# Window attention and a squared-ReLU feed-forward: three of four second-stage groups of the last pair of tiles as Strassen's seven products of 256 columns

## The chip, the cores and the metric

One core of one Trainium2 chip. The metric is device time in microseconds, here of that one core. The core's engines run side by side, each from its own queue in order: TensorE (PE, matmuls; PEld are its weight loads), VectorE (DVE), ScalarE (ACT), GpSimd (POOL), and SyncE (SP), which here issues every DMA.

## The reference

Windowed attention, then a feed-forward layer on its output, in float32:

```python
def _attn_ref(q, k, v):                      # 8 batches, 8 heads, 576 tokens, 64 wide; window 64
    scores = np.matmul(q, k.transpose(0, 1, 3, 2)) / np.sqrt(D)
    scores = np.where(mask, scores, -1e9)    # mask: 0 <= row - column < 64
    attn = np.exp(scores - np.max(scores, axis=-1, keepdims=True))
    attn = attn / (np.sum(attn, axis=-1, keepdims=True) + 1e-09)
    return np.matmul(attn, v)

def _moe_ref(x, w_in, w_out):                # x: 4608 x 512, w_in: 512 x 2048, w_out: 2048 x 512
    r = np.maximum(x @ w_in, 0.0)
    return (r * r) @ w_out
```

## The kernel before

**Tiles.** The 4608 tokens are 12 tiles of 384. float32 operands are split into a high part and a rest (`hi`, `lo`), and a product is three matmuls: hi by hi, hi by the other's rest, rest by hi. The first four tiles are computed plainly. The other eight are four pairs, j = 0 to 3, and the attention of a later pair runs beside the feed-forward of an earlier one; the last pair has no attention beside it.

**First stage of a pair** (x @ w_in): Strassen's scheme with seven products. `product(s, n)` (L896), s = 0 to 31, n = 0 to 6, eight steps s for a pair (`NP` = 8), does 6 matmuls of 384 columns into a PSUM bank of a ring of four (`bank`, L891, PSUM banks 4 to 7). DVE and ACT combine the seven sums into four blocks of g, and square them (`square`, L926; which engine does it stands in `SQUARES`, L956). The first half of the tokens lands in `g_first` (L618), a ring of three, the second half in `g_last` (L623), a ring of four in the slabs gb0 and gb1.

**Second stage** (g @ w_out): `second(k, x)` (L959) runs two steps behind. Two steps k, k + 1 make a group; an even k does the first half of the tokens for the group's 512 rows of w_out, an odd k the second. For each of three blocks x of 128 tokens: an ACT copy to `high(c)` (L609), a DVE subtraction to `low(c)` (L612), 12 matmuls of 512 columns into one bank (L991), and a DVE addition to `parts` (L602, by ACT's copy in the first group of a pair). `high` and `low` are thirds, 512 columns each, of the slabs hi and lo. The fourth group's sums go out by DMA (L1002).

**Weights.** `kept` and `mixed` are tensors in DRAM: the split weights, and Strassen's combinations of w_in, made by `mixing` (L841) ahead of the pairs. `wi_fetch` (L718) fetches 256 KB for a product into one of 13 slots, `wo_fetch` (L726) 512 KB of w_out into one of 8. Each waits, in SP's queue, until the slot is free and a tick (a product that PE has done) has come.

**Order.** `Plan` (L638) collects the operations with estimated costs, reads, writes and places. PE's order is that of the program. `in_order` (L655) orders the other engines' queues beforehand: at each point the ready operation with the earliest due time, which it counts back from PE's order. Waits at run time come from the data.

The main loop runs s = 0 to 33: products of s, fetches, then `second(s - 2, x)`, with bursts of attention between.

Of the kernel before, what the change touches and what calls it, by code (L numbers as in the profile page):

```python
# [8 lines left out]
F32 = mybir.dt.float32  # L9
F32R = mybir.dt.float32r  # L10
# [19 lines left out]
def window_attention_relu2_ffn(ctx: ExitStack, tc: tile.TileContext, q, k, v, w_in, w_out, out):  # L30
# [485 lines left out]
    mixed = dram.tile([NF // 2, P, 4, 2, 2 * P], F32, name="mixed")  # L516

# [118 lines left out]
    NP = NF // 2  # L636

# [88 lines left out]
    def wo_fetch(name, f, tick):  # L726
        n = wo_n[0]
        wo_n[0] += 1
        slot = n % NWO
        wo[name] = slot  # L730
        plan("sp", 0.4, lambda: sp.dma_start(wo_slot(slot).bitcast(F32), kept[f, :, 1]), tick, [("wo", slot)], 3.5,
             freed(f"wo{slot // 2}") if n < NWO else [], 1.4)
# [163 lines left out]
    def product(s, n):  # L896
# [20 lines left out]
        g11, g21 = ((lambda m=m: g_first(s % 3)[:, m], [("ga", s % 3, m)]) for m in range(2))  # L917
        g12, g22 = ((lambda m=m: g_last(s % 4)[:, m], [("gb", s % 4, m)]) for m in range(2))
        first_a = [("ghi", m) for m in range(3)] + [("glo", m) for m in range(2)] if s < 3 else []
        first_b = freed(f"gb{s % 4 // 2}") if s < 4 else []  # L920
# [16 lines left out]
        if n == 0:  # L937
            plan("act", 0.5, lambda: act.copy(sc(), b[0][:, :TT]), [b[1]], ["sc"], 0, first_s)
        elif n == 1:
            add(v, [kv], a[0][:, :TT], a[1], sc, "sc")  # L940
        elif n == 2:
            add(u, [ku], c[0][:, :TT], c[1], v, kv, first_s)
        elif n == 3:
            add(lambda: by_half(g22[0]()), g22[1], ordered(d[0][:, :TT]), d[1], lambda: ordered(u()), ku, first_b)
            square(g22, False, SQUARES[0])
        elif n == 4:
            plan("act", 0.5, lambda: act.activation(by_half(g11[0]()), ordered(a[0][:, :TT]), AF.Relu), [a[1]], g11[1], 0, first_a)  # L947
            square(g11, True, SQUARES[1])
        elif n == 5:
            add(lambda: by_half(g21[0]()), g21[1], ordered(c[0][:, :TT]), c[1], lambda: ordered(v()), kv, first_a)  # L950
            square(g21, False, SQUARES[2])
        elif n == 6:
            add(lambda: by_half(g12[0]()), g12[1], ordered(d[0][:, :TT]), d[1], lambda: ordered(v()), kv, first_b)
            square(g12, False, SQUARES[3])

    SQUARES = "dve", "pool", "pool", "dve"  # L956
    split_n = [0]

    def second(k, x):  # L959
# [3 lines left out]
        size, name = (4, "gb") if half else (3, "ga")  # L963
# [4 lines left out]
        def src():  # L968
            if half:
                g_last(slots[0])  # L970
                all4 = slabs[f"gb{slots[0] // 2}"][:, :4 * TT].rearrange("p (a b c) -> p a b c", a=2, b=2)
            else:
                g_first(0)
                all4 = xs["g"][:, slots[0]:slots[1] + 1:slots[1] - slots[0]]
            return all4[:, :, :, x * P:(x + 1) * P]
        g_keys = [(name, slot, m) for slot in slots for m in range(2)]
# [4 lines left out]
        plan("act", 0.62, lambda: act.copy(high(c), src()), g_keys, [kh], 0, freed("hi") if new else [])  # L981
        plan("dve", 0.7, lambda: dve.tensor_tensor(low(c), src(), high(c).bitcast(F32), ALU.subtract), g_keys + [kh], [kl], 0,
             freed("lo") if new else [])
# [9 lines left out]
        plan("pe", 2.59, do, [kh, kl] + [("wo", y) for y in w], [key])  # L993
# [10 lines left out]


# [31 lines left out]
    for s in range(NP * FULL + 2):  # L1037
        if s < NP * FULL:
            for mark in marks.get(2 * s, []):
                mark()  # L1040
            for n in range(7):
# [3 lines left out]
                if s % 2 == 0 and n % 2 == 0:  # L1045
                    f = s % NP * 2 + n // 2
                    wo_fetch((s // NP, f), f, [("tick", s, n)])
        if s >= 2:
# [45 lines left out]
```

## Time and profile before

| | |
|---|---|
| median of 3 runs | 849.41 us (848.75 to 849.77) |
| span of the profiled execution, first to last instruction | 847.5 us |
| PE busy | 830.3 us, 98% |
| DVE, ACT, POOL busy | 70%, 48%, 22% of the span |
| granted TensorE clock, mean | 0.998 |
| last pair of tiles | from 711.46 us |

The page gives no total for the profiled execution beside its span. PE counts as busy while a matmul is anywhere in its pipeline, so what a matmul costs is read from the time of a block divided by its matmuls, not from the mean duration of one. "Idle before" is the time in which the engine did nothing before the instructions of a group, with what ended it.

### The profile page before, as it was taken

What the parts mean: (1) busy time and instruction counts of PE and PEld (TensorE: products, weight loads), DVE (VectorE), ACT (ScalarE), POOL (GpSimd) and SP (SyncE); (2) the same over time, 40 slices, a digit from 0 to 9 for tenths busy, and PEclk for the clock granted to TensorE, in tenths of its full rate; (3) what the DMA queues carried; (4) which work ended last, traced back from release to release, by engine and by line L of the source; (5) the groups of instructions that cost most, each with busy time, mean ns of one, the idle gap of its engine ahead of it and who ended that gap; (6) DMA issues with size and microseconds to landing.
All of it is one profiled execution on the core that took longest, in us unless ns stands there. A gap on an engine that the chain in (4) does not pass through costs nothing.

```text
span 847.5 us, 17708 instructions
## 1 busy us (share of the span) xinstructions
PE 830.3 (98%) x6754; PEld 761.5 (90%) x6754; DVE 593.2 (70%) x888; ACT 406.3 (48%) x1130; POOL 184.4 (22%) x237
## 2 busy tenths in 40 slices
PE   7799999999999999999999999999999999999998
PEld 6678988989999999999999999999999999999997
DVE  4999996567766867867777765788755668544553
ACT  5896764645546554544452354353455324222221
POOL 1220003114457520311230121141112131011110
PEclk9999999999999999999999999999999999999999
DMA  9989954736698884998896797999785555776411
GB/s 225 225 250 360 306 238 77 146 84 173 175 191 265 216 178 111 296 255 209 185 323 240 172 220 159 281 230 264 219 235 151 195 189 179 242 256 213 133 69 75
DMA packets 273011, 173.92 MB, mean 205 GB/s; under 512 B 190496, under 2 KB 239648, under 8 KB 270880
## 3 DMA queue, kind: packets, MB, share of 16 engines
q1 hardware_dynamic: 272928, 172.80, 73.4%
q8 instruction: 53, 0.87, 0.4%
q14 instruction: 30, 0.25, 0.1%
HBM read 138.15 MB, written 34.60 MB: 204 GB/s over the span
## 4 chain that ended last, share of the span: by engine, by line
PE 86%; DVE 5%; DMA 3%; SPq 3%; ACT 2%; issue 1%; POOL 0%; DVEq 0%; ACTq 0%; POOLq 0%
PE banks L991 29%; PE banks L910 26%; PE banks L446 10%; PE banks L404 10%; PE banks L235 4%; PE banks L298 3%; SPq L147 3%; DMA w<-in_moe_w_out_dram 2%; PE banks L276 2%; DMA kept<-w 1%; PE banks L196 1%; DVE a L125 1%; DVE w L132 1%; DVE pt L280 1%; ACT a L118 1%
## 5 line engine op out<-in xcount | busy, mean ns | idle before, releaser
L991 PE MATMUL banks<-w 128*128 128x512 f32 x1152 | 257.5, 380 | 0.0
L991 PEld LDWEIGHTS banks<-w 128*128 128x128 f32 x1152 | 215.7, 189 | 28.4
L404 PE MATMUL banks<-x,w 128*128 128x384 f32 x768 | 138.1, 330 | 2.1 <-ACT r L413 2.0
L446 PE MATMUL banks<-w,g 128*128 128x512 f32 x576 | 136.4, 382 | 0.1
L404 PEld LDWEIGHTS banks<-x,w 128*128 128x128 f32 x768 | 126.7, 190 | 6.8 <-ACT r L413 3.6
L910 PE MATMUL banks<-x,w 128*128 128x384 f32 x768 | 130.3, 326 | 0.0
L936 POOL TENSOR_TENSOR g<-g 128x384 f32<-128x384 f32 x64 | 58.3, 913 | 324.4 <-ACT g L947 309.5
L910 PEld LDWEIGHTS banks<-x,w 128*128 128x128 f32 x768 | 125.6, 189 | 0.0
L446 PEld LDWEIGHTS banks<-w,g 128*128 128x128 f32 x576 | 106.2, 189 | 14.1 <-DVE g L423 0.9
L263 ACT ACTIVATE sel<-sel,nm 128x64 f32<-128x64 f32 x272 | 90.8, 336 | 23.1 <-DVE nm L257 22.8
L910 PE MATMUL banks<-w 128*128 128x384 f32 x576 | 100.7, 329 | 0.0
L999 DVE TENSOR_TENSOR w<-w,banks 128x512 f32<-128x512 f32 x72 | 49.5, 687 | 69.1 <-PE banks L991 69.1
L910 PEld LDWEIGHTS banks<-w 128*128 128x128 f32 x576 | 93.8, 189 | 1.9
L413 ACT ACTIVATE r<-banks 128x384 f32<-128x384 f32 x64 | 31.3, 489 | 71.9 <-PE banks L404 66.7
L981 ACT CAST w<-w 128x512 fp32r<-128x512 f32 x48 | 29.8, 620 | 72.9 <-PE banks L991 72.9
L272 POOL TENSOR_TENSOR sel<-sel,nm 128x512 f32<-128x512 f32 x33 | 36.0, 1091 | 109.6 <-ACT g L947 51.7
L981 ACT CAST w<-g 128x512 fp32r<-128x512 f32 x48 | 29.7, 621 | 62.1 <-PE banks L991 60.0
L263 ACT ACTIVATION_READ_ACCUMULATOR sel<-sel,nm 128x1 f32 x272 | 51.2, 188 | 0.0
L423 DVE TENSOR_TENSOR g<-r,g 128x384 fp32r<-128x384 f32 x64 | 37.2, 584 | 17.3 <-ACT g L421 11.3
L929 DVE SCALAR_TENSOR_TENSOR w<-w 128x384 f32<-128x384 f32 x64 | 46.8, 731 | 1.8
L924 DVE TENSOR_TENSOR w<-banks,r 128x384 f32<-128x384 f32 x64 | 38.6, 603 | 13.1 <-PE banks L910 12.9
L280 DVE TENSOR_TENSOR pt<-banks,masks 128x1024 f32<-128x1024 f32 x33 | 40.2, 1219 | 10.6 <-PE banks L276 10.6
(103 smaller groups left out, 970.6 us busy)
## 6 DMA issues: line engine op xcount, KB each, us to landing
w<-mixed SPq DMA_DIRECT2D x128, 256.0 KB, 5.2
w<-kept SPq DMA_DIRECT2D x64, 512.0 KB, 7.2
w<-kept SPq DMA_DIRECT2D x96, 256.0 KB, 5.7
kept<-w SPq DMA_DIRECT2D x16, 1024.0 KB, 9.2
vt<-in_v_dram SPq DMA_DIRECT2D x144, 64.0 KB, 3.1
w<-in_moe_w_in_dram SPq DMA_DIRECT2D x16, 512.0 KB, 7.2
w<-in_moe_w_out_dram SPq DMA_DIRECT2D x16, 512.0 KB, 8.1
raw<-in_q_dram SPq DMA_DIRECT2D x112, 72.0 KB, 3.1
```

What stands on the lines that cost most here:

```text
L263: act.activation(sels[i][:, w, hd], sels[i][:, w, hd], AF.Exp, bias=nms[i][:, n], scale=SCALE, accum_out=sums[i][:, n])
L280: dve.tensor_tensor(pts[i].rearrange("p (w n) q -> p w n q", n=2), ps_t[i][:, :, None, :].broadcast_to([P, SW, 2, P]), masks.rearrange("p ...
L404: pe.matmul(h_ps, lhsT=weights(kk, part), rhs=in_turn(x[xx][:, kk // 2, kk % 2]), start=n == 0, stop=n == 3 * NK - 1)
L423: (pool if eng == "p" else dve).tensor_tensor(gs[n][1], rg.pop(n), gs[n][0].bitcast(F32), ALU.subtract)
L446: pe.matmul(acc(t, tb), lhsT=gg[:, ts], rhs=in_turn(weights(part)), start=f == 0 and n == 0, stop=f == NF - 1 and n == 2)
L910: pe.matmul(ps[:, :TT], lhsT=w[:, part, kk * P:(kk + 1) * P], rhs=in_turn(x[:, xx, kk]), start=n < 4 and m == 0, stop=m == 5, skip_group_c ...
L924: plan("dve", 0.6, lambda: dve.tensor_tensor(to(), ps, other(), ALU.add), [kps, ko], keys, 0, after)
L929: plan("dve", 0.57, lambda: dve.scalar_tensor_tensor(x(), x(), 0.0, x(), ALU.max, ALU.mult), [], keys)
L936: plan("pool", 0.95, lambda: pool.tensor_tensor(x(), x(), x(), ALU.mult), [], keys)
L981: plan("act", 0.62, lambda: act.copy(high(c), src()), g_keys, [kh], 0, freed("hi") if new else [])
L991: pe.matmul(ps, lhsT=gg[:, m // 2, m % 2], rhs=in_turn(wo_slot(w[m])[:, part]), start=m == 0 and n == 0, stop=m == 3 and n == 2)
L999: plan("dve", 0.72, lambda: dve.tensor_tensor(by_half(parts(tb)), by_half(parts(tb)), ordered(ps), ALU.add), [key], [kp])
```

## The change

In the last pair (s = 24 to 31, `LAST` = 24), three groups (k = 24, 26, 28) no longer run `second`. `fast_half(k)` builds Strassen's operands from the 2 x 2 blocks of g (a11 and a12 the first half of the tokens, a21 and a22 the second): sums in the slab t (DVE three, POOL one), and for each of seven operands an ACT copy and a DVE subtraction of 768 columns into one of four sets of buffers (`side`; sets 0 and 1 lie in the slabs hi and lo, two others in tiles of the attention). `fast(k, m)` runs a product: 3 token blocks x 2 x 3 matmuls of 256 columns, into two PSUM banks of 0 to 3, which are evacuated into `total(m)`, by ACT's copy for k = 24, by a DVE addition after. Products 0 to 3 run after the products of s = k + 2, products 4 to 6 after those of s = k + 3. `fast_out` combines the seven totals into `parts` in s = 31, and the fourth group (k = 30, 31) is done by `second` as before, with its fetches of w_out ticked in s = 31 in place of s = 30. `mixing2(j, p, c)` makes w_out's combinations, by POOL, ACT and DVE, in pairs j = 1 and 2 (p = 0 to 5, c = 0, 1: twelve times) and writes them to `mixed2` in DRAM. `fast_fetch` fetches each product's weights, from `kept` by two DMAs or from `mixed2` by one. In the last pair `LAST_SQUARES` gives two of four squares to ACT in place of DVE, and `g_first` lies in the tile `wide`, a ring of four.

```diff
+    mixed2 = dram.tile([NF // 2, P, 4, 2, DM // 2], F32, name="mixed2")
...
+    def g_first(s):
+        return g_steps()[:, s % 3] if s < LAST else wide()[:, s % 4 // 2, s % 2]
...
+    LAST = NP * (FULL - 1)
+    SETS = 4
...
+    LAST_SQUARES = "act", "pool", "pool", "act"
...
+        dead = [(y, c) for y in ("shi", "slo") for c in range(2)] if k >= LAST else []
+        plan("act", 0.62, lambda: act.copy(high(c), src()), g_keys, [kh], 0, freed("hi") if new else dead)
...
+    def mixing2(j, p, c):
...
+        for f in range(2):
+            plan("pool", 0.81, by(whole, f), wo_keys([w[f]]), [("m2", f)])
+        both = [("m2", f) for f in range(2)]
+        for to, a, b in (((0, 0), (0, 1), (0, 0)), ((0, 1), (1, 1), (0, 1)), ((1, 1), (1, 1), (0, 0)), ((1, 0), (1, 1), (1, 0))):
+            plan("pool", 0.54, by(less, to, a, b), [], both, 1.0 if to == (1, 0) else 0.0)
+        plan("act", 0.62, lambda: act.copy(top(), scr()), both, ["m2hi"], 1.0)
+        plan("dve", 0.7, lambda: dve.tensor_tensor(scr().bitcast(F32R), scr(), top().bitcast(F32), ALU.subtract), ["m2hi"], both)
+        for part, x, keys in ((0, top, ["m2hi"]), (1, scr, both)):
+            plan("sp", 0.5, lambda part=part, x=x: sp.dma_start(
+                mixed2[p, :, :, part, c * P:(c + 1) * P], x().bitcast(F32).rearrange("p f l c -> p (f l) c")),
+                 keys, [("mixed2", p, c, part)], 4.5, (), 0.9)
+
+    FAST = ("A11", 0, 0), ("A12", 1, 0), ("A22", 2, None), ("S1", 0, None), ("S2", 3, None), ("S4", 1, 1), ("S3", 1, None)
...
+    def side(n):
...
+        if n < 2:
+            views = [slab(name, F32R)[:, n * 2 * TT:(n + 1) * 2 * TT] for name in ("hi", "lo")]
+        elif n == 2:
+            views = [xs[name][:, :2 * TT] for name in ("sel", "pt")]
+        else:
+            views = [xs["vt"][:, part * 2 * TT:(part + 1) * 2 * TT] for part in range(2)]
...
+        def split(name, x):
+            n = side_n[0] % SETS
...
+            plan("act", 0.84, lambda: act.copy(side(n)[0], x[0]()), x[1], [("shi", n)], 0, dead)
+            plan("dve", 0.97, lambda: dve.tensor_tensor(side(n)[1], x[0](), side(n)[0].bitcast(F32), ALU.subtract),
+                 x[1] + [("shi", n)], [("slo", n)], 0, dead)
+        split("A11", a11)
+        split("A12", a12)
+        split("A22", a22)
+        mixed_of("dve", t[0], a21, a22, ALU.add)
+        mixed_of("pool", t[1], a11, a21, ALU.subtract)
+        split("S1", t[0])
+        fast(k, 0)
+        mixed_of("dve", t[0], t[0], a11, ALU.subtract)
+        split("S2", t[0])
+        fast(k, 1)
+        mixed_of("dve", t[0], a12, t[0], ALU.subtract)
+        split("S4", t[0])
+        fast(k, 2)
+        split("S3", t[1])
+        fast(k, 3)
...
+    def fast(k, m):
...
+        pair = fast_n[0] % 2
+        fast_n[0] += 1
+        ps = banks[:, 2 * pair:2 * pair + 2].rearrange("p a b -> p (a b)")[:, :2 * TT]
...
+            for x in range(NTB):
+                c = 0
+                for st in range(2):
+                    for gg, part in ((hi, 0), (hi, 1), (lo, 0)):
+                        pe.matmul(ps[:, x * 2 * P:(x + 1) * 2 * P], lhsT=gg[:, st, x * P:(x + 1) * P], rhs=in_turn(w[:, st, part]),
+                                  start=c == 0, stop=c == 5, skip_group_check=True)
+                        c += 1
...
+        if k == LAST:
+            plan("act", 0.84, lambda: act.copy(total(m), ps), keys, to, 0,
+                 QK_KEYS if m < 6 else [("ga", n, y) for n in range(3) for y in range(2)])
+        else:
+            plan("dve", 0.97, lambda: dve.tensor_tensor(total(m), total(m), ps, ALU.add), keys, to)
...
+        write("pool", 0, 0, M1, M2, ALU.add)
+        inside("dve", M6, M1, ALU.add)
+        inside("pool", M3, M5, ALU.add)
+        write("dve", 0, 1, M6, M3, ALU.add)
+        inside("dve", M7, M6, ALU.add)
+        write("dve", 1, 0, M7, M4, ALU.subtract)
+        write("dve", 1, 1, M7, M5, ALU.add)
+
+    FAST_FIRST = 4
+    FAST_END = NP * FULL - 2
...
-                if s % 2 == 0 and n % 2 == 0:
...
+                if s < LAST and s % 2 == 0 and n % 2 == 0 or s == FAST_END + 1 and n % 2 == 0:
...
+                if s > LAST and s % 2 and n % 2 == 0 and s < FAST_END:
+                    fast_fetch(s - 1, n // 2, [("tick", s, n)])
+                if s > LAST + 1 and s % 2 == 0 and n % 2:
+                    fast_fetch(s - 2, FAST_FIRST + n // 2, [("tick", s, n)])
+        if LAST + 2 <= s < FAST_END + 2:
+            if s % 2 == 0:
+                fast_half(s - 2)
+            else:
+                for m in range(FAST_FIRST, 7):
+                    fast(s - 3, m)
+            if s == FAST_END + 1:
+                fast_out()
+        elif s >= 2:
+            if NP + 2 <= s < NP * 3 + 2 and (s - 2) % NP < NP - 2:
+                mixing2((s - 2) // NP, (s - 2) % NP, (s - 2) // NP - 1)
```

## Rows read from the trace of the kernel before

**Rows 1.** The page: busy time, share of the span and instructions of each engine, and the granted clock of PE in 40 slices, in tenths.

```profile
PE 830.3 (98%) x6754; PEld 761.5 (90%) x6754; DVE 593.2 (70%) x888; ACT 406.3 (48%) x1130; POOL 184.4 (22%) x237
...
PEclk9999999999999999999999999999999999999999
```

**Rows 2.** The chain of waits of the last pair of tiles, in order of time: start, duration, what, how many.

```profile
711.46 6.83 PE banks L910 x42
718.28 7.77 PE banks L991 x36
...
820.45 23.32 PE banks L991 x108
...
843.79 0.69 DVE w L999
```

**Rows 3.** A window of two steps in the last pair, k = 24 in the second stage: from and to, length, busy time of PE, PEld, DVE, ACT and POOL (with instructions), granted clock, DMA share and GB/s.

```profile
740.65:769.84 29.19, 29.19 (x158) 27.26 (x158) 13.73 (x21) 8.87 (x17) 3.32 (x4) 1.00 0.63 207
```

**Rows 4.** Groups by line and shape of PE and PEld in the last pair, 711.46 to 843.8 us: busy time, mean ns of one, idle time before.

```profile
L991 PE MATMUL banks<-w 128*128 128x512 f32 x360 | 79.0, 379 | 0.0
...
L991 PEld LDWEIGHTS banks<-w 128*128 128x128 f32 x360 | 67.8, 189 | 9.2
```

**Rows 5.** Matmuls of 128 columns: the timeline of PE's warm-up matmuls from 11.7 us (start, duration from the first one's start to the last one's end, count), their loads and matmuls by line (ns, least, median, most), and four transposes from the chain of waits.

```profile
11.48 1.95 PE L512 MATMUL banks<-ident 128*128 128x128 f32 x16
...
L512 PEld LDWEIGHTS banks<-ident x58: 190/192/333, 1.5 to 24.3; 128*128 128x128 f32 x58
L512 PE MATMUL banks<-ident x58: 273/275/579, 1.5 to 24.4; 128*128 128x128 f32 x58
...
643.67 0.44 PE banks L276 x4
```

**Rows 6.** Groups by line and shape of DVE and ACT in the last pair.

```profile
L999 DVE TENSOR_TENSOR w<-w,banks 128x512 f32<-128x512 f32 x25 | 17.2, 688 | 31.2 <-PE banks L991 31.2
L929 DVE SCALAR_TENSOR_TENSOR w<-w 128x384 f32<-128x384 f32 x18 | 12.4, 690 | 0.6
L982 DVE TENSOR_TENSOR w<-w 128x512 fp32r<-128x512 f32 x15 | 10.3, 686 | 6.0 <-ACT w L981 6.0
L924 DVE TENSOR_TENSOR w<-banks,r 128x384 f32<-128x384 f32 x16 | 9.7, 608 | 5.0 <-PE banks L910 5.0
...
L924 DVE TENSOR_TENSOR g<-banks,r 128x384 f32<-128x384 f32 x8 | 5.2, 648 | 5.7 <-PE banks L910 5.7
L924 DVE TENSOR_TENSOR w<-banks,w 128x384 f32<-128x384 f32 x8 | 5.2, 648 | 2.9 <-PE banks L910 2.9
L924 DVE TENSOR_TENSOR r<-banks,w 128x384 f32<-128x384 f32 x8 | 4.5, 558 | 4.2 <-PE banks L910 4.0
...
L981 ACT CAST w<-w 128x512 fp32r<-128x512 f32 x15 | 9.3, 620 | 24.3 <-PE banks L991 24.3
...
L932 ACT ACTIVATE g<-g 128x384 f32<-128x384 f32 x8 | 4.2, 525 | 9.3 <-DVE g L924 9.3
```

**Rows 7.** Operations of 768 columns: groups of DVE, ACT and POOL from 380 to 711 us; and, from the timelines of DVE and POOL, a DVE operation that begins while POOL squares.

```profile
L874 DVE TENSOR_TENSOR w<-a,w 128x768 fp32r<-128x768 f32 x6 | 5.7, 949 | 0.0
...
L873 ACT CAST x<-w 128x768 fp32r<-128x768 f32 x6 | 5.0, 834 | 0.2
...
L862 POOL TENSOR_TENSOR w<-a,w 128x768 f32<-128x768 f32 x3 | 5.5, 1831 | 0.2
...
705.16 1.58 DVE L862 TENSOR_TENSOR w<-a,w 128x768 f32<-128x768 f32 x1
...
705.06 0.86 POOL L936 TENSOR_TENSOR g<-g 128x384 f32<-128x384 f32 x1 [1.28 <-ACT g L932]
```

**Rows 8.** Windows, columns as in rows 3: the densest stretch of DVE, and steps 10 to 15 (pair j = 1) and 18 to 23 (pair j = 2).

```profile
437.00:453.00 16.00, 16.00 (x89) 15.03 (x88) 15.48 (x23) 7.99 (x13) 2.30 (x2) 1.00 0.68 210
483.00:566.00 83.00, 83.00 (x693) 76.59 (x690) 57.54 (x94) 37.31 (x126) 19.60 (x18) 1.00 0.84 218
614.00:697.00 83.00, 83.00 (x700) 76.53 (x693) 49.91 (x84) 35.14 (x112) 18.53 (x17) 1.00 0.63 197
```

**Rows 9.** Timeline: the start of the last plain blocks on PE with the first copy and addition behind them, and a wait of PE for an evacuation by ACT earlier in the run.

```profile
820.28 23.47 PE L991 MATMUL banks<-w 128*128 128x512 f32 x108
...
822.91 0.62 ACT L981 CAST w<-g 128x512 fp32r<-128x512 f32 x1 [2.20 <-PE banks L991]
823.07 0.69 DVE L999 TENSOR_TENSOR w<-w,banks 128x512 f32<-128x512 f32 x1 [1.04 <-PE banks L991]
...
189.11 0.49 ACT L413 ACTIVATE r<-banks 128x384 f32<-128x384 f32 x1 [2.31 <-PE banks L404]
...
189.65 0.76 PE L404 MATMUL banks<-x,w 128*128 128x384 f32 x3 [0.58 <-ACT r L413]
```

**Rows 10.** Groups of POOL over the whole span: the sums of `mixing`, of 256 and 128 columns.

```profile
L539 POOL TENSOR_TENSOR a<-a 128x128 f32<-128x128 f32 x56 | 29.3, 541 | 1.4
L535 POOL TENSOR_TENSOR a<-w 128x256 f32<-128x256 f32 x28 | 25.0, 909 | 99.5 <-DVE w L132 73.7 <-DVE a L543 25.7
...
L535 POOL TENSOR_TENSOR w<-w 128x256 f32<-128x256 f32 x4 | 2.9, 731 | 2.0 <-DVE w L543 1.5 <-PE banks L446 0.5
```

**Rows 11.** DMA: issues of w_out's fetches from 711.46 to 828 us (count, KB each, median us from issue to landing), and what SP's queue waited for before a w_in fetch from 430 to 844 us (us in total, times, longest).

```profile
w<-kept SPq DMA_DIRECT2D x16, 512.0 KB, 7.0
...
SPq L723 <- PE banks L910: 133.7, 76, 10.9
```

More of the change, by code (lines that the diff above doesn't have):

```diff
@@ L971, in src @@
                 all4 = slabs[f"gb{slots[0] // 2}"][:, :4 * TT].rearrange("p (a b c) -> p a b c", a=2, b=2)
-            else:
-                g_first(0)
-                all4 = xs["g"][:, slots[0]:slots[1] + 1:slots[1] - slots[0]]
+            elif k >= LAST:
+                all4 = wide()[:, slots[0] // 2]
+            else:
+                all4 = g_steps()[:, slots[0]:slots[1] + 1:slots[1] - slots[0]]
             return all4[:, :, :, x * P:(x + 1) * P]
-        g_keys = [(name, slot, m) for slot in slots for m in range(2)]
+        g_keys = [key for s in pairs for m in range(2) for key in ([("gb", s % 4, m)] if half else g_first_keys(s, m))]
         c = split_n[0] % 3
@@ L1002, in second, with whole, less @@
             plan("sp", 0.4, lambda: sp.dma_start(out[row:row + P, :], parts(tb)), [kp], [], 3.0, (), 0.7)
+    def mixing2(j, p, c):
+        w = [wo[j, 2 * p + f] for f in range(2)]
+        scr = lambda: slab("gb0", F32)[:, 3 * DM:].rearrange("p (f l c) -> p f l c", f=2, l=2)
+        top = lambda: slab("gb1", F32)[:, 3 * DM:].bitcast(F32R).rearrange("p (f l c) -> p f l c", f=2, l=2)
+        def whole(f):
+            hi, lo = (wo_slot(w[f])[:, part].bitcast(F32).rearrange("p (l c) -> p l c", l=2)[:, :, c * P:(c + 1) * P]
+                      for part in range(2))
+            pool.tensor_tensor(scr()[:, f], hi, lo, ALU.add)
+        def less(to, a, b):
+            x = scr()
+            pool.tensor_tensor(x[:, to[0], to[1]], x[:, a[0], a[1]], x[:, b[0], b[1]], ALU.subtract)
+        for f in range(2):
[9 more added lines that the diff above has]
+                 keys, [("mixed2", p, c, part)], 4.5, (), 0.9)
@@ new lines, in window_attention_relu2_ffn, with fast_fetch @@
+    FAST = ("A11", 0, 0), ("A12", 1, 0), ("A22", 2, None), ("S1", 0, None), ("S2", 3, None), ("S4", 1, 1), ("S3", 1, None)
+    def fast_fetch(k, m, tick):
+        p = k % NP
+        name, kind, half = FAST[m]
+        if half is None:
+            source = [mixed2[p:p + 2, :, kind].rearrange("s p h e -> p s (h e)")]
+            keys = [("mixed2", p + n, c, part) for n in range(2) for c in range(2) for part in range(2)]
+        else:
+            source = [kept[2 * (p + n) + kind, :, 1, :, half * 2 * P:(half + 1) * 2 * P] for n in range(2)]
+            keys = []
+        wo_fetch(("fast", k, m), source, whole_slot if half is None else both_slot, keys + tick)
```

104 lines of the change are left out of this document (87 added, 17 removed).

## The prediction

> **What bounds it now.** I read the engine shares and slices first: TensorE (PE) is busy 98% of the span at full granted clock [rows 1]. Then the chain of waits over the last pair of tiles: from 711.46 us it holds matmuls alone, products (L910) and second-stage blocks (L991) in turn, until 843.77, with one VectorE (DVE) add and the output's DMA behind [rows 2]. A window of two steps agrees: PE busy 29.19 of 29.19 us, DVE 47%, ScalarE (ACT) 30%, GpSimd (POOL) 11% [rows 3]. So in this stage the time is the number of matmuls times their spacing. A block of 36 matmuls takes 7.77 us, 215.8 ns each; 42 products take 6.83 us, 162.5 ns each [rows 2]. That is (215.8 - 162.5)/128 = 0.416 ns a column plus some 2.5 ns. The groups by line show no idle time of PE in this stretch, and a weight load of 189 ns for each matmul [rows 4].
>
> **Part 1, fewer columns (removes PE time).** A group (two steps s) had 2 x 3 x 12 = 72 matmuls of 512 columns; it gets 7 products x 3 token blocks x 6 = 126 of 256. Three groups: 216 x 215.8 ns = 46.61 us go, 378 matmuls come. By columns one would take 256 x 0.416 + 2.5 = 109.2 ns. But each brings a load of 128 weight columns, and the question is how densely loads can follow. No row has this shape; the nearest have 128 columns behind 128x128 loads, in which the load must set the pace: 0.44 us for four transposes (109 ns), and the sixteen warm-up matmuls, with loads of 190 to 192 ns like ours, (1950 - 275)/15 = 111.7 ns [rows 5]. So 109.2 to 111.7; I take 110.5: 41.77 us, a saving of **4.84 us** (4.39 to 5.33). The 189 ns of a load is no spacing: at 162.5 ns apart loads already overlap one another [rows 2, 4].
> The same rows speak against a rule of the Trainium skill, "TensorE: Matmul & The Clock Gate", section "The mechanism": a load overlaps matmuls in flight only when it goes to another row group. All loads here use all 128 rows, and 162.5 ns for 384 columns leaves no room for a load in series: the trace disagrees. What it would make of the time is rival C.
>
> **Part 2, the new elementwise work (hidden, if DVE keeps up).** Per step DVE keeps five adds, 2 x 0.608 + 2 x 0.648 + 0.558 = 3.07 us [rows 6]. Per group it loses six splits and six adds of 0.69 and four squares (L929, 0.69) [rows 6], and gets 7 splits, 3 sums and 7 accumulations of 768 columns: 17 x 0.95 = 16.2 us, from the split of 768 columns [rows 7]; an accumulation out of PSUM I price by L999, 0.688 + 256 x 1.02 ns = 0.95 as well. Together 22.3 us in a group that now takes PE 13.66 + 13.92 = 27.6 us: 81%. ACT: per step three passes and two squares of two, at most 7 x 0.525 = 3.7; 7.4 + 7 copies x 0.835 = 13.2 us, and in the first group 7 evacuations at the same price, 19.1 us: at most 69% [rows 6, 7]. POOL: 4 x 0.86 + one sum of 1.83 = 5.3 us [rows 7]. Sums fit, and density alone does no harm: from 437 to 453 us DVE is busy 97% while PE never idles [rows 8].
> The tight place is PSUM. A product of the new kind uses two banks, and there are two such pairs, so product m+2 waits for the evacuation of product m. That starts 0.20 us after the last slot (slots of L991 end at 822.87, L999 starts at 823.07) [rows 9], takes 0.95, and PE goes on 0.05 us behind an evacuation (189.60, 189.65) [rows 9]: 1.20 of the 1.99 us that product m+1 lasts. One DVE operation already running costs up to 0.95 of the 0.79 left, so it makes PE late by 0.16 at most; two make it late by up to 1.1. Per group three evacuations are so placed (0 to 2, 1 to 3, 4 to 6); the others have a step's seven products between. In the four-product half DVE has to do about seven operations in 6 us, among them the chain t0, S2, S4. I take 0.3 to 0.4 us in all nine (three of them ACT's, k = 24), bounds 0 and 2.0 (most of them late by a quarter operation). **Cost 0.35 us.**
> DVE and POOL also get into each other's way: a DVE operation of 768 columns begun while POOL squares takes 1.58 instead of 0.95 us [rows 7]. With POOL busy 19% and ten such operations a group, that is about 10 x 0.19 x 0.6 = 1 us of DVE time a group, 84% in place of 81%; it is within the bounds above. The Trainium skill has this rule, "SBUF — State Buffer", section "Who interferes with whom": a VectorE operation with two inputs in SBUF and a GpSimd operation reading SBUF exclude each other for a whole instruction; the trace agrees (1.58 against 0.95 us).
>
> **Part 3, the way back to plain blocks (a new stall).** second(30, 0) copies g into high(0), in slab hi, columns 0 to 511. The seventh product of k = 28 has its operand in side 0 (side_n is 20 there), columns 0 to 767 of hi and lo. So the copy can't start before fast(28, 6) has read its weights; then come copy, subtraction and PE, with nothing else queued on PE. Let E be the end of the last slot. ACT starts at E + 0.04 (as L981 does) and takes 0.62; matmuls 1 and 2 run from E + 0.82, with 0.05 of hop and 0.11 for the load. DVE first evacuates fast(28, 6), E + 0.20 to 1.15, then subtracts until 1.84; matmul 3 starts at E + 2.0 where it would have at 0.43 [rows 5, 6, 9]. **Cost 1.6 us**; 1.1 with DVE free, 2.5 with one more operation of fast_out ahead of it. Behind it are 15.5 us of plain blocks, in which DVE has 12 x 0.69 and 5 us of fast_out to do, and the end (last add, output DMA) stays as it is.
>
> **Part 4, w_out's combinations (hidden).** Twelve times, in six steps of each of pairs 2 and 3: POOL 2 x 0.73 to 0.91 + 4 x 0.54 = 3.6 to 4.0 us [rows 10], ACT 0.62, DVE 0.69, and two output DMAs of 256 KB on SP's queue, each behind the DVE subtraction that it waits for, with weight fetches queued behind it. The cover: those stretches of 83 us have DVE at 69% and 60%, ACT at 45% and 42%, POOL below 24% [rows 8]. In pair 2 a seventh of a step's DVE slack is used. For DMA, 218 GB/s at a share of 0.84 is 260 GB/s when full; 0.52 MB more a step is 2.0 us of some 16.6, so 0.84 becomes 0.96, and 0.63 becomes 0.8. That is the thin cover. But SP spends 133.7 us, 76 times, waiting for PE to free a slot before a fetch [rows 11]: fetches run ahead as far as slots allow, and a landing that is 2 us later is absorbed. Cost 0, bounds 0 and 1.5 us (some fetches late). A gain is excluded, as PE waits for nothing there.
> In the last pair SP's queue gets 21 fetches of 512 KB for 12, nine of them as two DMAs. Each is ticked some 19 us before its product (about seven products of either kind and, where they lie between, three or four of the other) against a landing of 7.0 us [rows 11]. The tightest are the four for k = 30, now ticked in s = 31: the last has three products, nine plain matmuls and the stall of part 3, 6.0 + 1.9 + 1.6 = 9.5 us. Cost 0, bound 1 us.
>
> **The sum.** 4.84 - 0.35 - 1.6 = 2.9 us off. The profiled execution shows its span, 847.5 us; the median of the three runs is 849.41, 1.9 us above it, which lies outside the program and isn't touched. 849.41 - 2.9 = **846.5 us**. Bounds together: from 5.33 - 1.1 = 4.2 us off (845.2) to 2.5 + 2.0 + 1.5 + 1 - 4.39 = 2.6 us more (852.0), which needs all at once.
>
> **Rivals.** *A: the gain is eaten by the evacuations.* Each of nine tight evacuations late by 0.2 to 0.4 us, or the chain t0, S2, S4 late for its product: 2 to 3.5 us in place of 0.35, so 848.0 to 849.6. For it: 84% load, in bursts above 100%, and an order fixed beforehand; against: DVE at 97% stalled nothing [rows 8]. Chance 0.25.
> *B: slower, DVE sets the pace of the fast products.* If in the order of DVE one full operation stands ahead of each evacuation besides the one running, PE waits 1.1 us at nine places: 9.9 us, 9.9 + 1.6 - 4.84 = 6.7 us slower, 856.1. PE waits from an evacuation that starts over 1.0 us behind its product, and from 1.6 us at all nine places the kernel is slower by 0.2%. The planner takes the nearest due time first, which speaks against it. Chance 0.08.
> *C: slower, loads don't hide at 256 columns.* If a load must be over (189 ns) before its matmul, 378 x 189 = 71.4 us, 24.8 more than the old blocks, 876 us with part 3; if it runs in series with the columns, 109 + 109 = 218 ns, 82.4 us, 887 us. Against both are the 109 to 111.7 ns [rows 5]. Chance 0.03. The second case is what the rule of the Trainium skill named in part 1 would give.
> *D: fetches late in pairs 2 and 3* through DMA at 0.96: 1 to 3 us, 847.4 to 849.4. Chance 0.05.
> That the change doesn't do what it says can't well be: the counts stand in the loops.
>
> **How the numbers follow.** Forecast (845.2 to 847.7) 0.59, A 0.25, B 0.08, C 0.03, D 0.05. A measurement of this kernel can tell about 0.2%, 1.7 us: below 847.7 is faster, above 851.1 slower. Faster: forecast and a little of D, 0.61; same: A and most of D, 0.28; slower: B and C, 0.11. Leaving out C, B's upper part and the corner below 845.0, the range is 845.0 to 850.5 us.
>
> **What would show it.** PE's 256-column matmuls 109 to 112 ns apart; one PE wait of about 1.6 us (in one or two pieces) ahead of the plain blocks of k = 30, put down to ACT or DVE (w, L981 or L982 as they were); waits of 0.1 to 0.2 us, if any, between products, put down to the accumulation; pairs 2 and 3 as long as before. It is wrong if the spacing is above 115 ns, if products wait for more than 0.3 us each, or if PE waits for a DMA before 711 us.

## The result, and the profile after

The changed kernel took **855.43 us** (median of six runs, 854.24 to 859.24) against 849.48 us (six runs, 848.75 to 850.36): a ratio of 1.0072, 95% interval 1.0054 to 1.0089. It is slower by 0.7%; the forecast was 2.9 us faster, with a range that ended at 850.5 us.

The page of the changed kernel, the lines that answer to [rows 1]:

```profile
PE 830.9 (97%) x6916; PEld 766.0 (90%) x6916; DVE 620.5 (73%) x905; ACT 435.5 (51%) x1178; POOL 243.9 (29%) x314
...
PEclk9799999999999999999999999999999999999999
```

PE's busy time is nearly the same (830.9 for 830.3 us), though 162 more matmuls run; the span is 5.2 us longer. So PE waits more. Where it does is read from the start of each step's first product in both timelines, after minus before. Three stretches hold everything:

| stretch | after minus before |
|---|---|
| up to the first product of s = 0 (335.14 us before) | +1.76 us |
| steps 0 to 26, in pieces: 11 to 12 +0.44, 13 to 14 +3.78, 14 to 15 +1.40, 16 to 17 +0.65; else 0.00 | +6.28 us |
| from s = 26 to the end, the last pair's fast groups and the way back | -2.82 us |

**The last pair** did what was forecast. Its chain of waits in the changed kernel (start, duration, what, how many), beside [rows 2]; L932 is the product matmul, L1151 the new 256-column matmul, L1019 the plain block:

```profile
748.68 6.83 PE banks L932 x42
755.51 8.04 PE banks L1151 x72
763.54 6.83 PE banks L932 x42
770.37 6.03 PE banks L1151 x54
...
825.81 6.04 PE banks L1151 x54
831.85 0.03 issue
831.88 0.95 DVE g L1160
832.83 0.61 DVE w L1010
833.44 0.04 issue
833.49 15.39 PE banks L1019 x70
```

Four products take 8.04 us where a block took 7.77, three take 6.03: 111.6 ns a matmul. Three groups take 42.2 us in place of 46.6, 4.4 us less. There is no wait between them: the chain changes from L932 to L1151 and back without a gap. In the windows of the three groups (columns as in [rows 3]) DVE is busy 60 to 75%, below the 81% of the forecast:

```profile
748.50:776.20 27.70, 27.70 (x211) 27.68 (x210) 16.63 (x22) 16.79 (x27) 5.86 (x5) 1.00 0.86 281
776.20:804.00 27.80, 27.80 (x213) 27.80 (x213) 20.50 (x26) 13.01 (x22) 5.14 (x5) 1.00 0.83 261
804.00:832.20 28.20, 27.88 (x213) 27.69 (x211) 20.94 (x27) 10.84 (x20) 7.45 (x6) 1.00 0.52 165
```

**Pairs 2 and 3** hold the loss. What PE waited for over the whole span, of the kinds that grew there (us in total, times, longest), before,

```profile
PE banks L298 <- DVE pt L280: 3.4, 3, 1.6
...
PE banks L276 <- POOL sel L272: 0.9, 1, 0.9
```

and after:

```profile
PE banks L298 <- DVE pt L280: 4.5, 3, 1.7
PE banks L276 <- POOL sel L272: 3.9, 3, 2.2
...
PE banks L932 <- DVE r L949: 0.6, 2, 0.4
```

L276 is the attention's transposes, waiting for POOL, L298 the attention's product with v, waiting for DVE. From 430 to 720 us PE waited for nothing before and 4.6 us after, in five waits of these three kinds. The rest of the 6.28 us isn't idle time: part of it is that the matmul behind a block no longer overlaps the block's end (before, it started 5.18 us after a block of 24 did; that block ends at 5.34 us), and 0.44 us, at steps 11 to 12, is another matter, told below under rival D. POOL's own waits from 430 to 720 us that ended with a write:

```profile
POOL w L1042 <- DMA mixed<-w: 70.4, 8, 17.8
```

And one of ACT's in the same stretch:

```profile
ACT w L1052 <- POOL w L1046: 13.6, 5, 7.7
```

L1042 and L1046 are POOL's six sums in `mixing2`, L1052 its ACT copy, L1055 its two writes to `mixed2` (the profile calls that tensor `mixed`). Before, none of POOL's waits in that stretch ended with a DMA. Now the first sum of a combination stands at the head of POOL's queue for 70 us in all, in eight of the twelve, waiting until the write of the combination before has landed: there is one scratch for all twelve. The timeline around the worst of them (start, duration, engine, line; in brackets the idle time before and what ended it):

```profile
537.70 0.57 SPq L1055 DMA_DIRECT2D mixed<-w  x1
...
543.13 5.34 PE L1019 MATMUL banks<-w 128*128 128x512 f32 x24
...
546.16 1.41 POOL L1042 TENSOR_TENSOR w<-w 128x256 f32<-128x256 f32 x2 [17.81 <-DMA mixed<-w]
...
547.53 2.05 POOL L1046 TENSOR_TENSOR w<-w 128x128 f32<-128x128 f32 x4
...
549.54 1.04 POOL L272 TENSOR_TENSOR sel<-sel,nm 128x512 f32<-128x512 f32 x1
549.62 0.62 ACT L1052 CAST w<-w 128x512 fp32r<-128x512 f32 x1 [7.75 <-POOL w L1046]
550.14 0.52 ACT L957 ACTIVATE g<-g 128x384 f32<-128x384 f32 x1
...
550.64 0.66 PE L276 MATMUL banks<-ident,sel 128*128 128x128 f32 x4 [2.17 <-POOL sel L272]
```

Read it from the top. SP issues the write at 537.70; in the chain of waits its piece lasts 8.33 us, to 546.03. POOL, which had been idle for 17.81 us, runs the six sums, and only then L272, the attention's normalisation. PE has finished its block at 548.5 and stands until 550.64, 0.06 us behind L272. ACT stood behind the same sums for 7.75 us, its next square (L957) behind the copy.

### The profile page after: what moved, and what is told of

Its sections match the earlier page's. It is cut to its first block, busy times and chain, and to the rows that moved or that the text cites. A ratio compares the mean times of both kernels' runs of the same rounds, so it can differ in the third digit from the quotient of the medians.

```text
span 852.7 us, 18273 instructions
## 1 busy us (share of the span) xinstructions
PE 830.9 (97%) x6916; PEld 766.0 (90%) x6916; DVE 620.5 (73%) x905; ACT 435.5 (51%) x1178; POOL 243.9 (29%) x314
## 4 chain that ended last, share of the span: by engine, by line
PE 79%; DVE 7%; DMA 3%; SPq 3%; POOL 3%; issue 2%; ACT 2%; DVEq 0%; POOLq 0%; ACTq 0%
PE banks L932 23%; PE banks L1019 20%; PE banks L446 11%; PE banks L404 11%; PE banks L1151 5%; PE banks L235 3%; PE banks L298 3%; SPq L147 2%; PE banks L276 2%; DMA vt<-in_v_dram 1%; DVE w L132 1%; DVE a L123 1%; DMA mixed<-w 1%; PE banks L196 1%; DVE a L125 1%
## 5 line engine op out<-in xcount | busy, mean ns | idle before, releaser
L1019 PE MATMUL banks<-w 128*128 128x512 f32 x936 | 210.4, 381 | 0.9 <-DVE w L1010 0.6
L1019 PEld LDWEIGHTS banks<-w 128*128 128x128 f32 x936 | 174.9, 189 | 24.4 <-DVE w L1010 1.0
L932 PE MATMUL banks<-x,w 128*128 128x384 f32 x768 | 130.9, 326 | 0.6 <-DVE r L949 0.6
L932 PEld LDWEIGHTS banks<-x,w 128*128 128x128 f32 x768 | 125.5, 189 | 1.3 <-DVE r L949 1.2
L932 PE MATMUL banks<-w 128*128 128x384 f32 x576 | 100.7, 329 | 0.0
L932 PEld LDWEIGHTS banks<-w 128*128 128x128 f32 x576 | 93.4, 189 | 1.6
L961 POOL TENSOR_TENSOR g<-g 128x384 f32<-128x384 f32 x48 | 47.7, 997 | 155.5 <-ACT g L972 145.4
L1027 DVE TENSOR_TENSOR w<-w,banks 128x512 f32<-128x512 f32 x60 | 41.0, 686 | 42.0 <-PE banks L1019 42.0
L272 POOL TENSOR_TENSOR sel<-sel,nm 128x512 f32<-128x512 f32 x33 | 36.4, 1102 | 68.4 <-DVE nm L269 41.9
L536 POOL TENSOR_TENSOR a<-w 128x256 f32<-128x256 f32 x28 | 25.0, 909 | 99.5 <-DVE w L132 73.8
L1009 ACT CAST w<-w 128x512 fp32r<-128x512 f32 x39 | 24.2, 620 | 56.7 <-PE banks L1019 56.6
L418 DVE TENSOR_TENSOR r<-r 128x384 f32<-128x384 f32 x38 | 24.9, 655 | 27.4 <-ACT r L413 27.3
```

The costliest lines, as they stand in the source:

```text
L272: (dve if eng == "d" else pool).tensor_tensor(p, p, rs[i][:, :, None].broadcast_to([P, SW * 2, QB]), ALU.mult)
L932: pe.matmul(ps[:, :TT], lhsT=w[:, part, kk * P:(kk + 1) * P], rhs=in_turn(x[:, xx, kk]), start=n < 4 and m == 0, stop=m == 5, skip_group_c ...
L961: plan("pool", 0.95, lambda: pool.tensor_tensor(x(), x(), x(), ALU.mult), [], keys)
L1019: pe.matmul(ps, lhsT=gg[:, m // 2, m % 2], rhs=in_turn(wo_slot(w[m])[:, part]), start=m == 0 and n == 0, stop=m == 3 and n == 2)
L1027: plan("dve", 0.72, lambda: dve.tensor_tensor(by_half(parts(tb)), by_half(parts(tb)), ordered(ps), ALU.add), [key], [kp])
```

## The experiments

Every kernel starts from the changed one. The kernel before gave medians of 850.4 to 851.4 us beside them, so ratios are compared, and from the profiles the three stretches of the table above (us):

| kernel | median us | ratio to before, 95% | start | steps 0 to 26 | s = 26 to end |
|---|---|---|---|---|---|
| changed | 855.43 | 1.0072 (1.0054 to 1.0089) | +1.76 | +6.28 | -2.82 |
| e_nomix | 847.12 | 0.9958 (0.9946 to 0.9971) | +0.33 | 0.00 | -2.52 |
| e_alone | 858.01 | 1.0082 (1.0069 to 1.0095) | +1.94 | +6.33 | +0.02 |
| e_nodma | 854.82 | 1.0044 (1.0030 to 1.0058) | +2.15 | +7.60 | -2.82 |
| e_lands | 857.32 | 1.0074 (1.0060 to 1.0089) | +2.62 | +0.54 | +5.76 |
| e_tick | 854.04 | 1.0034 (1.0022 to 1.0047) | +0.52 | +5.85 | -2.83 |
| e_nodma_tick | 847.98 | 0.9965 (0.9951 to 0.9978) | +2.22 | 0.00 | -2.83 |
| e_double | 860.98 | 1.0123 (1.0104 to 1.0142) | +1.49 | +8.71 | -2.83 |
| e_best | 857.20 | 1.0069 (1.0051 to 1.0088) | +0.14 | +8.00 | -4.31 |
| e_spread | 853.97 | 1.0043 (1.0030 to 1.0055) | -0.11 | +8.46 | -4.31 |
| e_lands7 | 858.13 | 1.0090 (1.0075 to 1.0106) | +1.85 | +0.88 | +5.90 |
| e_gap | 846.39 | 0.9950 (0.9935 to 0.9965) | +1.04 | +0.01 | -4.30 |
| e_gap8 | 845.62 | 0.9946 (0.9931 to 0.9961) | +0.45 | 0.00 | -4.31 |
| e_nomix_side | 846.94 | 0.9953 (0.9939 to 0.9966) | +1.61 | 0.00 | -4.00 |

In e_double and e_best the profiled execution is the fastest of its runs, 4 us below the median, so their stretches hold less than the ratio says. The expectations of e_nodma, e_lands, e_lands7, e_double and e_spread missed, and that of e_best in its total; e_nomix_side lies just outside its range.

**First the two halves of the change.** e_nomix leaves out `mixing2`:

```diff
-                mixing2((s - 2) // NP, (s - 2) % NP, (s - 2) // NP - 1)
+                pass
```

> The last pair as changed, w_out's combinations not made in pairs 2 and 3 (their products read w_in's combinations from DRAM instead, so the output of three groups is another). Theory (POOL's queue stands behind the landing of the combinations' writes): pairs 2 and 3 take as long as before the change, the 6.3 us lost between products 11 and 17 are gone, the last pair stays 2.8 us shorter: 846.7 us, or 848.5 if the 1.8 us lost in the first 50 us belong to the program. The rivals on work and on DMA traffic say the same; a rival on the planner (another order in pairs 2 and 3 because the last pair is another) says 853 or more.

e_alone keeps `mixing2` and runs the last pair as before (`LAST = NP * FULL`, no fast groups).

> w_out's combinations made and written in pairs 2 and 3, the last pair computed as before the change (so the combinations are used by nothing). All theories that put the loss on the combinations: before plus 6.3 us, 855.8 us, plus 1.8 if the start belongs to the program. The rival on the planner: 849.5.

The table answers: without `mixing2` steps 0 to 26 lose nothing and the last pair gains 2.5; with `mixing2` alone they lose 6.33 and the last pair is as before. In the stretches the two halves add up (6.33 and -2.52 us against 6.28 and -2.82). In the medians they do so only roughly: the two ratios multiply to 1.0040, the change as made has 1.0072, and the start of the run, which scatters by 2 us (see the last part of the account below), is in each of them. The loss in steps 0 to 26 is `mixing2`'s.

**What in it: sums, writes or waits?** e_nodma drops the 24 writes and keeps the sums (the loop over `sp.dma_start` is out, the last pair fetches from `mixed`).

> The combinations computed by POOL, ACT and DVE as in the changed kernel, their 24 writes to DRAM left out (products read w_in's combinations instead, so the output of three groups is another). Theory: nothing lands, so POOL never waits for it: 846.7 to 848.5 us, as without the combinations. Rival work (the sums themselves keep POOL, ACT and DVE busy, or DVE and POOL exclude each other): the loss stays, 853 or more. Rival traffic (writes delay the fetches of weights): 846.7 to 848.5.

The theory that only the landing of writes holds POOL fell here: without any, 7.6 us were lost in one place. Timeline of e_nodma:

```profile
536.15 3.19 PE L932 MATMUL banks<-w 128*128 128x384 f32 x18
...
538.24 0.73 POOL L1042 TENSOR_TENSOR w<-w 128x256 f32<-128x256 f32 x1 [9.93 <-DMA w<-kept]
...
543.91 0.62 ACT L1052 CAST w<-w 128x512 fp32r<-128x512 f32 x1 [7.82 <-POOL w L1046]
...
544.96 0.49 ACT L963 COPY w<-banks 128x384 f32<-128x384 f32 x1
...
545.49 0.56 DVE L949 TENSOR_TENSOR r<-banks,w 128x384 f32<-128x384 f32 x1 [0.23 <-ACT w L963]
...
546.10 4.74 PE L932 MATMUL banks<-x,w 128*128 128x384 f32 x18 [5.79 <-DVE r L949]
```

The sum now waits for its source, w_out's fetch (`w<-kept`); the plan reckons 3.5 us for such a landing, and the median in e_nodma, from 430 to 720 us, is 7.0. ACT's queue waits behind the sum (L1052), with a product's copy out of PSUM (L963) queued behind that; DVE's addition waits for the copy, and PE for the bank, 5.79 us (of the rest of the 7.60, 1.55 us lie in the 18 matmuls behind it, which take 4.74 us where 18 took 3.19; see the last section). It is the same chain with another DMA at its head. (The Trainium skill, "PSUM — Partial Sum Buffer", section "Engine vs sequencer instructions", has the queues of ACT, DVE and POOL strictly first in, first out. The trace agrees: L963, whose product is among the matmuls that had ended by 539.34, starts at 544.96, 0.43 us after the copy L1052 ends, and not before.)

e_tick lets the first sum wait, in the plan, for the first product of its step, so that it is ordered behind work of a later time; e_nodma_tick does both:

```diff
-            plan("pool", 0.81, by(whole, f), wo_keys([w[f]]), [("m2", f)])
+            plan("pool", 0.81, by(whole, f), wo_keys([w[f]]) + [("tick", s, 0)], [("m2", f)])
```

> The changed kernel with one more condition on POOL's first sums of a step: not before the first product of that step, so some 30 us behind the issue of the fetch whose slot they read. Theory now (POOL's queue, then ACT's, stand behind any DMA that lands later than the planner reckoned: the combinations' own write, and the fetch of w_out): POOL's waits for fetches go, those for the landing of the last write of a single scratch remain at least in part; pairs 2 and 3 lose between 0 and 6 us, PE's waits there named POOL, DVE or ACT. Rival work (the sums' own time): 6 us lost as in the changed kernel.

> The same condition, and the 24 writes left out (products read w_in's combinations, so the output of three groups is another): all of the sums' work, and nothing that it has to wait for. Theory: pairs 2 and 3 lose less than 0.5 us, 0.996 of before (2.8 us less, as without the combinations). Rival work: 4 us or more lost in pairs 2 and 3, slower than before.

e_tick and e_nodma_tick differ in the writes, and in what the last pair then fetches. Without the writes all of the sums, copies and subtractions run, and steps 0 to 26 lose 0.00 us. So the work itself can be hidden, as forecast, and the rival that it crowds POOL, ACT and DVE is dead. With the tick alone (writes on) 5.85 us are lost, and no sum waits for a fetch any more; what is left is `POOL w L1042 <- DMA mixed<-w`, 63.3 us in eight waits.

**Telling the planner how long a landing takes.** The plan reckons 4.5 us for a write; e_lands says 10.0, e_lands7 (with the tick) 7.5.

> The changed kernel with one number of the planner changed: it reckons 10.0 us in place of 4.5 from the issue of such a write to its landing, so that it places the next sums later in POOL's queue, behind the squares and the attention's products. All work and all DMAs stay. Theory: POOL's waits for landings shrink from 70 us to a few, and PE's waits in pairs 2 and 3 with them: 847 to 849 us. Rival work: 853 or more. Rival traffic: 853 or more, with PE waiting for weights.

> The changed kernel with the condition on POOL's first sums (not before the first product of their step), and the planner reckoning 7.5 us in place of 4.5 to a write's landing (between the changed kernel's number and the 10.0 that made the last combinations late for the last pair). Theory: POOL's waits for landings shrink but the single scratch stays, pairs 2 and 3 lose 0 to 2 us, no wait of PE for weights in the last pair: 0.997 to 0.9995 of before. Rival traffic or work: 1.003 or more.

Both took most of the loss out of pairs 2 and 3 (0.54 and 0.88 us left) and both lost it again in the last pair: twelve combinations, each waiting longer in the plan, no longer end in time. What PE waited for in e_lands:

```profile
PE banks L1151 <- DMA w<-mixed: 6.8, 1, 6.8
```

The last sums ran from 750.1 to 754.3 us; in the chain of waits the fetch of a product's weights, into a slot of w_out that these sums read, follows one of them at 753.05 and lands 8.3 us later. In e_lands7 it is the same, at 752.74.

**A second scratch.** e_double gives every even p a scratch in the slab t.

> All work and all writes, with the condition, and with two scratch sets in turn (the second in the slab t, free in those steps), so that a write has a step more to land before POOL needs its scratch. Theory: pairs 2 and 3 lose less than 1 us, 0.996 to 0.998 of before. Rival work: as the changed kernel, slower than before. Rival traffic (24 writes delay fetches): PE waits for DMA of w in pairs 2 and 3.

In the profiled execution steps 10 to 15 lose nothing, but 6.4 us are lost at steps 15 to 17 and 2.3 at 23 to 25: there slab t is wanted for the operands of the next pair, whose first sum on POOL (L884) then waits for a write to land. POOL's wait in e_double:

```profile
POOL w L884 <- DMA mixed<-w: 10.1, 2, 5.5
```

And PE's, behind the split of these operands:

```profile
PE banks L932 <- DVE w L896: 2.6, 1, 2.6
PE banks L932 <- ACT w L895: 1.6, 1, 1.6
```

e_best also lets the operands' sets start with the third (`n = (side_n[0] + 2) % SETS`), so that the last one isn't in the slabs hi and lo.

> As the run with two scratch sets, and the four operand buffers of the last pair taken in turn from the third on, so that the seventh product of k = 28 no longer lies in the slabs hi and lo and the copy for the first plain block waits for the sixth product. Theory: PE's stall ahead of the plain blocks (0.48 + 0.80 + two of 0.10 us after the change) is gone, 1.3 to 1.5 us less than the run before, some 4 us under before. If the stall has another cause than the buffer, it stays.

The loss in pairs 2 and 3 stayed (8.00 us; there the profile puts L884's waits down to other releasers than a write). The stall ahead of the plain blocks went: from s = 26 to the end -4.31 in place of -2.83 us, so that stall was worth **1.48 us**.

e_spread keeps both edits and deals the twelve out anew: two in pair 1, and four of them (s = 11, 13, 19, 21) with slab t as scratch.

> All work and all writes of the changed kernel; the twelve combinations placed so that the scratch in the g slabs is used in every second step at most, the scratch in slab t only in steps 11, 13, 19 and 21 (two steps ahead of its next use for the operands), two combinations already in pair 1 (steps 5 and 7); POOL's first sums not before the first product of their step; operand buffers of the last pair from the third on. Theory (only waits for landings at the head of POOL's queue cost): pairs 1 to 3 as long as before, the last pair 4.2 to 4.4 us shorter: 0.9950 of before (0.9945 to 0.9960). Rival traffic: 24 writes still delay something, 0.998 or more.

One loss of 8.46 us, again a write's landing: the writes from slab t went out at 552.04, and L884 ran at 558.73. The timeline of e_spread:

```profile
552.04 1.25 SPq L1058 DMA_DIRECT2D mixed<-w  x2
...
558.73 1.81 POOL L884 TENSOR_TENSOR w<-a 128x768 f32<-128x768 f32 x1 [16.50 <-ACT sel L263]
...
568.92 1.11 PE L276 MATMUL banks<-ident,sel 128*128 128x128 f32 x4 [5.60 <-POOL sel L272]
569.68 5.12 PE L1019 MATMUL banks<-w 128*128 128x512 f32 x12
```

The profile names ACT for L884, but that had long been done; the landing is inferred: in the changed kernel such writes take 5.7 us in the median from issue to landing. PE waits 5.60 us behind it.

**Room for each landing.** e_gap puts the twelve at every second step, from pair 1 on, with the scratch in t only in steps 12 and 20, three steps ahead of its next use for the operands; tick and operand sets are as in e_spread:

```diff
...
+    UNITS = {3: (0, 0), 5: (2, 0), 7: (4, 0), 9: (0, 1), 11: (1, 0), 12: (2, 1), 13: (3, 0), 15: (5, 0),
+             19: (1, 1), 20: (3, 1), 21: (4, 1), 23: (5, 1)}
...
-            if NP + 2 <= s < NP * 3 + 2 and (s - 2) % NP < NP - 2:
-                mixing2((s - 2) // NP, (s - 2) % NP, (s - 2) // NP - 1)
+            if s in UNITS:
+                mixing2((s - 2) // NP, *UNITS[s], s)
```

> All work and all writes. The twelve combinations in steps 3, 5, 7, 9, 11, 13, 15, 19, 21, 23 with the scratch in the g slabs (never in two steps running) and in steps 12 and 20 with the scratch in slab t, three steps ahead of its next use; POOL's first sums not before the first product of their step; operand buffers from the third on. Theory (landings at the head of POOL's queue are the whole loss): pairs 1 to 3 lose under 1 us, 0.9950 to 0.9965 of before. Rival traffic (the writes by themselves): 0.999 or more, with PE waiting for weights or POOL for fetches.

e_gap8 plans 9.0 us for the landing as well. e_nomix_side is e_nomix with the sets started at the third: what is left if `mixing2` cost nothing at all.

> The same places, and the planner reckoning 9.0 us in place of 4.5 to a write's landing, so that what reads the scratch next is put later in POOL's queue. Theory: as e_gap or better, 0.9950 to 0.9960. Rival traffic: 0.999 or more.

> The last pair alone: combinations left out (products read w_in's in their place, output of three groups another), operand buffers from the third on, so that the stall ahead of the plain blocks goes. All theories: 1.4 to 1.5 us under the run without the combinations, 0.9940 to 0.9950 of before.

e_gap does all the work and all the writes, loses 0.01 us in steps 0 to 26 and stands at 0.9950, e_gap8 at 0.9946, beside the bound (e_nomix_side, 0.9953) no different within the intervals (the 0.3 us between -4.00 and -4.31 lie behind the start of the last products). POOL still waits for writes in e_gap8, but from 330 to 850 us PE then waits for nothing; and the plain blocks follow the products at once. POOL's wait, from 330 to 720 us:

```profile
POOL w L1045 <- DMA mixed<-w: 18.0, 2, 15.5
```

And the end of the chain of e_gap8:

```profile
818.23 6.03 PE banks L1154 x54
824.26 15.56 PE banks L1019 x72
```

So e_gap8 computes what the kernel before does and is 0.54% faster than it, and some 1.25% faster than the change as made (0.9946/1.0072). With all 24 writes on and nothing lost, traffic has no price here either.

**The pace of the new matmuls.** e_narrow is e_nomix with 192 columns to a fast matmul (a quarter of each product's columns left out), one run.

> As the run without the combinations, and each of the 378 matmuls has 192 columns in place of 256 (a quarter of the columns of the three groups isn't computed, their output is another). If the weight load sets the pace, as the 111.6 ns measured at 256 columns and the 111.7 ns of the 128-column warm-up suggest, the spacing stays 111.6 ns and the time 847. If columns set it, 192 x 0.416 + 2.5 = 82.4 ns, 11 us less: 836.

Chain of waits of e_narrow:

```profile
746.89 8.01 PE banks L1151 x72
...
761.75 6.00 PE banks L1151 x54
```

111.2 ns at 192 columns, 111.6 at 256: a quarter fewer columns change nothing, so columns don't set the pace. What is left in each pair is its load of 128 columns. It is not the bare number of instructions: in the attention 32 pairs of 64x64 go by in 1.00 us (L235 in the changed kernel). No run changed the load alone.

## Why the prediction was wrong

**What failed is one step: part 4, "w_out's combinations (hidden)", "Cost 0, bounds 0 and 1.5 us".** It cost 6.3 us in the profiled execution. The sizes in it were right: 48 sums of 128 columns at 559 ns and 24 of 256 at 779 make 3.8 us each time, as forecast (3.6 to 4.0), and e_nodma_tick shows that work hidden in full. Wrong was the question asked. The step compared busy shares with what POOL, ACT and DVE had left over 83 us (which hold five of a pair's six steps, s = 10 to 14 and 18 to 22), and DMA's share with its limit. But the new operations wait: for a fetch of w_out, and for the write of the combination before to leave the one scratch. The waits stand in queues that run in order, with L272 behind POOL's and squares and PSUM copies behind ACT's, and PE behind those. POOL was busy 33% of the window from 491 to 566 us in the changed kernel, and PE stood behind it all the same:

```profile
491.00:566.00 75.00, 71.37 (x621) 64.69 (x620) 48.92 (x80) 34.87 (x120) 24.56 (x31) 1.00 0.84 224
```

In the text the waits named were SP's: "two output DMAs of 256 KB on SP's queue, each behind the DVE subtraction that it waits for". The wait in the other direction, POOL for the DMA, was in the code (the key `m2` that the second write holds and the next first sum takes) and was not followed. Following it could have given the place and the doubt: the plan counts 4.5 us for a landing, [rows 11] show 7.0 for a fetch, so a first sum can be 2.5 us late, twelve times, with whatever is urgent on POOL and ACT behind it.

**Rival D**, "fetches late in pairs 2 and 3", had the place and a DMA, but not the mechanism: the DMA share was 0.84 in pair 2, as before [rows 8], and PE waited for a fetch once: at 518.89 us a weight load of the attention (L298) waits 0.25 us for v, and its block of 32 takes 1.39 in place of 0.95 us. These are the 0.44 us at steps 11 to 12; e_alone, with all the writes, doesn't have them. The sentence on what would refute the prediction, "if PE waits for a DMA before 711 us", catches only this: in the rest PE waited for POOL, and POOL for the DMA. The sign that did fail is "pairs 2 and 3 as long as before".

**The other terms.** Part 1: 111.6 ns, at the upper bound (111.7, taken from sixteen warm-up matmuls) and not 110.5: 4.4 in place of 4.84 us. Part 2: 0 in place of 0.35; rivals A and B have no wait in the trace that would speak for them. The slowing of DVE beside POOL is there, and larger than the 1.58 us of [rows 7]: three splits that begin beside POOL's sums take 1.81 to 1.87 us (at 773.98, 801.01 and 817.88), most others 0.95. In the trace the evacuations out of PSUM, beside such sums at 800.14 and 817.01, stay at 0.95. It fits in the slack. Part 3: forecast 1.6, and the third plain matmul starts 2.05 us after the end of the last slot, if that lies 0.04 ahead of ACT's start as the forecast put it (2.0 forecast); e_best gives 1.48 back. The timeline of the changed kernel there:

```profile
831.48 1.66 ACT L1009 CAST w<-a 128x512 fp32r<-128x512 f32 x3 [3.92 <-PE banks L1151]
831.88 0.95 DVE L1160 TENSOR_TENSOR g<-g,banks 128x768 f32<-128x768 f32 x1 [1.06 <-PE banks L1151]
...
832.16 0.70 PE L1019 MATMUL banks<-w 128*128 128x512 f32 x2 [0.32 <-ACT w L1009]
832.75 1.89 DVE L1010 TENSOR_TENSOR w<-a,w 128x512 fp32r<-128x512 f32 x3
833.49 2.86 PE L1019 MATMUL banks<-w 128*128 128x512 f32 x12 [0.63 <-DVE w L1010]
```

As forecast, ACT's copy waits for the products, DVE's evacuation goes ahead of its subtraction. Rival C is refuted by the pace. So the last pair came out at -2.8 us (forecast 2.9 off) by luck in the sizes: 0.45 us less gained in part 1, 0.35 and some 0.1 less lost in parts 2 and 3.

**Not settled: the first 335 us**, where the profiled execution lost 1.76 us. Windows of 20 to 40 us: before,

```profile
20.00:30.00 10.00, 7.31 (x144) 5.98 (x144) 9.97 (x13) 9.21 (x36) 2.16 (x4) 1.00 1.15 234
30.00:40.00 10.00, 7.62 (x108) 6.53 (x108) 9.75 (x16) 8.15 (x26) 3.27 (x3) 0.83 0.82 199
```

and after:

```profile
20.00:30.00 10.00, 7.73 (x119) 6.63 (x112) 9.87 (x14) 9.18 (x39) 2.33 (x4) 0.83 0.99 230
30.00:40.00 10.00, 7.55 (x141) 6.33 (x134) 9.39 (x12) 7.65 (x26) 2.70 (x3) 0.68 0.88 203
```

The granted clock (the last column but two) was 1.00 and 0.83 before, 0.83 and 0.68 after. The column "start" of the table runs from -0.11 to +2.62 us over kernels that do the same there, and it goes with the clock: from 20 to 50 us the mean granted clock is 0.94 in the kernel before and in the four where the column is below 0.5 (e_nomix, e_best, e_spread, e_gap8), 0.89 in three with 0.52 to 2.22, and 0.83 in the seven with 1.49 to 2.62. The kernel before has both by itself: over its runs beside the experiments it takes 848.5 to 850.5 us where the mean clock of the run is 0.998, and 850.4 to 852.2 where it is 0.994 or less. So this scatter is there without the change. All six runs of the changed kernel have 0.992 to 0.995, so up to 2 us of the 5.95 between the medians can be of this kind. Whether the change makes the longer start more frequent, and what decides it, no run shows.

## What to carry to other kernels

Where work is put into a queue that runs in order, ask first what it waits for and what stands behind it, and only then how busy the engine is: here twelve times 3.8 us of work that can be hidden cost 6.3 us in all, because of a buffer that a DMA had to leave. An operation that reuses the source of a DMA write carries that write's landing (5.7 us in the median of pairs 2 and 3 here, 8.3 in the case shown) to the head of its queue; give it another buffer that nobody urgent shares, or a step of its own in between. A change of the planned duration alone moved the loss here: with less room than the landings need, it came out at the end (e_lands, 5.76 us).

## What was not expected of the hardware

A stream of loads and matmuls runs at 111 to 112 ns a pair whether the matmul has 128, 192 or 256 columns ([rows 5], e_narrow, the change): with a load of 128 columns to each, products narrower than 256 columns have nothing more to give. The Trainium skill, "TensorE: Matmul & The Clock Gate", section "LDWEIGHTS (loading the stationary operand)", gives columns / 1.2 ns for a load, 106.7 ns for 128; the measured pace, 111.2 to 111.7 ns, is 4.5 to 5 ns above that.

A wait on PE can cost more than itself. In e_spread the twelve matmuls after the wait of 5.60 us took 5.12 us, 427 ns each instead of 215.8, at a granted clock of 0.66 in that window, that is partly at the lower of the two levels (1.2 GHz):

```profile
566.00:576.00 10.00, 7.08 (x25) 6.08 (x26) 2.47 (x4) 1.38 (x3) 4.97 (x8) 0.66 0.94 207
```

Of its loss of 8.46 us, some 2.5 us (12 x 211 ns) are this. e_nodma shows 0.66 too from 540 to 550 us, where its wait of 5.79 us lies. In the changed kernel, with waits up to 2.2 us, the window of 491 to 566 us shows 1.00.
